# Moving the transposes of an attention pair behind the scores of the next pair in a fused attention and MLP kernel

## The chip, the cores and the metric

The kernel runs on one core of a Trainium2 chip. Its metric is the device time of one execution in microseconds (us), and a kernel's time is the median of several executions. Here the three of the kernel before are 601.35, 600.53 and 597.79 us, so the median is 600.53 us.

## The reference, cut to what matters

Three layers follow each other. The change touches the first alone.

```python
# attention: q, k, v are (2, 8, 768, 64); n_sink 4, window 128
scores = scale * q @ k.T
scores = where(is_sink | in_window, scores, -1e9)
a = exp(scores - max); a = a / (sum(a) + 1e-9)
attn = a @ v                      # per batch and head
x = attn -> (2, 768, 512)
# layer 2, with a layer norm ahead
xn = (x - mean) / sqrt(var + 1e-6) * g_ln
x = x + relu(xn @ w_ch1) @ w_ch2  # 512 -> 2048 -> 512
# layer 3: theta = x @ w_theta, cos and sin, two token mixes, w_ch
```

## The kernel before, in words

The 1536 tokens are cut into six pieces of 256 tokens (two tiles of 128). A row of a tile attends to its own tile, to the tile before and to 16 sink columns. Attention runs per piece over four pairs of heads, as a Python generator that the rest of the kernel advances step by step. Its steps are:

- S, the scores (`scores`, L264): per tile one product for each of the two heads, into two PSUM banks.
- the mask with the row's extremum on VectorE (L378), and the exponential with its row sum on ScalarE (L381), into the tile p.
- T, the transposes (`turn_w`, L428), on TensorE: p is turned into the bank wp, and then ScalarE (L431) and VectorE (L432) split it into two fp16 parts wt. For a piece that has sinks, `turn_sinks` turns 16 more columns (L441, L445, L446).
- F, the product with v (`values`, L464), into the bank pv, which VectorE scales into x (L481).

I write S(2,3) for the scores of heads 2 and 3, and T4 or F4 for the transposes and the product of head 4. Only pieces 0 and 1 (below `TURNED`) are turned on TensorE. The later pieces are turned by the DMA queue and the change leaves them alone.

When all heads of piece 0 are done, VectorE forms the layer norm (`norm`: L580, L591, L595, L598), TensorE turns it (`norm_T`, L611), and layer 2 begins. It goes by units: unit u multiplies with the u-th 128 columns of the first weight (`first`, L645) and the u-th rows of the second (`second`, L692). In units 0 to 7 only piece 0 takes part, in plain fp32, and the attention of piece 1 is interleaved with them. From unit 8 piece 1 joins (L666), which needs its own layer norm.

Weights arrive as 64-bit words, 1 MB per unit. `load_w12` loads f0, f1, f2 and so on (L547) into one of two raw buffers. It turns them into fp32 by L551 and L555 on VectorE and L552 and L554 on ScalarE. A buffer is free for the load after next once its L555 is done. f3 therefore waits for f1's L555, and f4 for f2's.

TensorE's order is the order of the Python code (a manual schedule). On VectorE, ScalarE and the DMA-issuing engine SP a scheduler sets the order when the program is built, by its own times. An engine works through its rows in that order. PSUM has few banks for this: in the units two for S, one for wp and one for pv. The tiles p have four buffers and the q and k tiles two.

Of the kernel before, what the change touches and what calls it, by code (L numbers as in the profile page):

```python
# [19 lines left out]
B, H, S, D = 2, 8, 768, 64  # L20
# [26 lines left out]
READY1 = 5.5  # L47
READY2 = 13.0
RATE = 7.0
PRE = [12, 17, 21]  # L50
AHEAD = (4, 4)
START = 2
EARLY = 38.0
# [14 lines left out]
class Net:  # L68
# [197 lines left out]
    def attn_fast(self, eng):  # L266

        steps = [(piece, h) for piece in range(NP) for h in range(H)]
        nc, p, qk, scored, turned, sent, late = self.nc, self.att, {}, [], [], [], []

        def load(j, eng=eng):
            if j < len(steps):
                piece, h = steps[j]
                if h % 2 == 0:
                    qk[piece, h] = qk[piece, h + 1] = self.split_qk(piece, h // 2, eng)

        def load_v(piece):
            if piece < NP:
                b, tiles = self.tiles(piece)
                for t in ([tiles[0] - 1] if tiles[0] else []) + tiles + ([NT] if tiles[-1] >= 2 else []):  # L280
                    self.split_v(b, t)

        def ahead(piece):
            return self.tc.high_priority() if piece < TURNED else ExitStack()

        def turn():

            piece, h, pt, st = scored.pop(0)
            b, tiles = self.tiles(piece)
            with ahead(piece):  # L290
                blocks = self.turn_w(pt, tiles)
            sinks = None
            if tiles[0]:
                sinks = []
                if not turned:

                    pool, tag = self.vbanks[self.vturn % len(self.vbanks)]
                    self.vturn += 1
                    with ahead(piece):
                        self.turn_sinks(pool.tile([128, 512], F32, tag=tag, name="pv"), pt, sinks)  # L300
            turned.append((piece, h, blocks, sinks, st, pt))

        def finish(head):

            piece, h, blocks, sinks, st = head[:5]
            b, tiles = self.tiles(piece)
            with ahead(piece):
                self.values(b, h, tiles, piece, blocks, sinks, st, turned[0] if turned and turned[0][3] is not None else None)
                if h % (H // 2) == H // 2 - 1:
                    self.stats(piece, h // (H // 2))  # L310
            if h == V_RANGE:
                while late:
                    q, ts = self.tiles(late.pop())
                    for t in ts:
                        with self.behind():
                            self.range_v(q, t)
            if h == H - 1:
                with ahead(piece):
                    self.norm(piece)
                late.append(piece)  # L320

        load(0, self.nc.vector)
        load_v(0)
        for j, (piece, h) in enumerate(steps):
            if h % 2:
                continue
            b, tiles = self.tiles(piece)
            if h == 0:
                self.x[piece] = self.new_x(piece)
            load(j + 2)  # L330
            if h == 2:
                load_v(piece + 1)
            pair = yield from self.softmax(b, (h, h + 1), tiles, qk[piece, h])
            if piece >= TURNED:
                if len(sent) >= LAG:
                    for _ in range(2):
                        finish(sent.pop(0))
                for h, pt, st in pair:
                    sent.append((piece, h) + self.send_w(pt, tiles) + (st,))
                yield  # L340
                continue
            for h, pt, st in pair:
                scored.append((piece, h, pt, st))
                turn()
                yield
                if len(turned) > 2:
                    finish(turned.pop(0))
                    yield
            if h == H - 1:

                while turned:
                    finish(turned.pop(0))
                    yield
        while sent:
            yield
            finish(sent.pop(0))
        for t in tiles:
            self.range_v(b, t)
# [457 lines left out]
    def run(self, general):  # L816
# [47 lines left out]
        while 0 not in self.xnorm:  # L864
            next(side)
            n += 1
            if n == 1:
                self.late()
            if n in PRE and not general:
                with self.behind():  # L870
                    self.load_w12(PRE.index(n))
        if general:
            for f in range(len(PRE)):
                self.load_w12(f)
# [220 lines left out]
```

## Time and profile before

| what | us |
|---|---|
| median of three executions | 600.53 |
| the profiled execution's own time | 601.21 |
| its span, first to last instruction | 599.4 |
| until layer 2 begins (L645 of unit 0) | 48.60 |
| until piece 1 joins (first L666) | 123.65 |

The profiled execution lies 0.7 us above the median, inside the spread of the three. A row of the timeline gives start, duration, engine, line, operation, output and inputs, shapes and count. In brackets stands the time that the engine was idle before it, and who ended that. A row of the waits gives the sum, the number and the longest. A row of grouped instructions gives busy time and the mean of one in ns, then the idle time before them by releaser.

### The profile page before, as it was taken

Reading aid. Unit: us, or ns where it says so; the run is one execution under the profiler, and the core shown is the slowest. Engines: PE = TensorE matmul, PEld = TensorE weight load, DVE = VectorE, ACT = ScalarE, POOL = GpSimd, SP = SyncE. Lnnn points to the kernel's source line nnn. Section 1 sums busy time; section 2 is a strip of 40 time slices with the busy share of each in tenths; the row PEclk is TensorE's granted clock in tenths of the full one; section 3 lists DMA queues with packets and bytes.
Section 4 is the critical chain, followed back from the end, with each engine's and each line's share of the span. In section 5 each row is a group of like instructions: output and inputs, shape, how many; then the busy total and the mean of one; then the engine's idle time right before and its main releaser. Section 6 shows DMA issues by size and latency. Waiting matters only on the chain.

```text
span 599.4 us, 9411 instructions
## 1 busy us (share of the span) xinstructions
PE 545.5 (91%) x3545; PEld 449.0 (75%) x3545; DVE 407.5 (68%) x902; ACT 336.2 (56%) x719; POOL 60.9 (10%) x53
## 2 busy tenths in 40 slices
PE   3646887889999999999999899999999899999995
PEld 1424454567777777777888688888999799999995
DVE  5773557789987897787666643557988789754161
ACT  4755666699765775666446533347676566433020
POOL 1000000000000000000022200002333333310000
PEclk9999889999999999999999799999999799999998
DMA  7461545389632456223412210001313311001112
GB/s 251 166 236 56 200 165 188 109 202 220 116 89 50 104 117 102 45 44 46 114 36 100 95 52 1 1 1 54 105 62 119 110 54 64 13 25 35 37 37 76
DMA packets 54536, 55.37 MB, mean 92 GB/s; under 512 B 39760, under 2 KB 42832, under 8 KB 54480
## 3 DMA queue, kind: packets, MB, share of 16 engines
q1 hardware_dynamic: 54480, 54.67, 31.7%
q8 instruction: 30, 0.49, 0.3%
q14 instruction: 26, 0.21, 0.1%
HBM read 42.08 MB, written 3.15 MB: 75 GB/s over the span
## 4 chain that ended last, share of the span: by engine, by line
PE 65%; DVE 13%; DMA 10%; ACT 8%; issue 3%; POOL 1%; SPq 0%; DVEq 0%; ACTq 0%; POOLq 0%
PE acc L692 18%; PE h L666 16%; PE m L777 12%; DMA raw<-w 5%; PE f L808 5%; PE th L736 3%; PE pv L464 3%; PE s L264 3%; ACT raw L552 2%; PE h L645 2%; DMA raw<-wtok 1%; DVE w L555 1%; ACT w L554 1%; DVE st L555 1%; DMA raw<-wth 1%
## 5 line engine op out<-in xcount | busy, mean ns | idle before, releaser
L634 DVE TENSOR_TENSOR wl<-w,wh 128x512 fp32r<-128x512 f32 x96 | 68.9, 721 | 48.8 <-ACT wh L633 25.9
L633 ACT ACTIVATE wh<-w 128x512 fp32r<-128x512 f32 x96 | 59.8, 627 | 72.3 <-PE acc L692 45.6
L666 PE MATMUL h<-xT,wh 128*128 128x512 f32 (+1 forms) x384 | 93.1, 379 | 0.5 <-ACT p L381 0.5
L666 PEld LDWEIGHTS h<-xT,wh 128*128 128x128 f32 x384 | 66.9, 188 | 14.4 <-ACT p L381 0.7
L692 PE MATMUL acc<-wh,hh 128*128 128x512 f32 x176 | 72.9, 414 | 0.0
L692 PE MATMUL acc<-wl,hh 128*128 128x512 f32 x176 | 69.9, 397 | 0.0
L692 PE MATMUL acc<-wh,hl 128*128 128x512 f32 x176 | 69.8, 397 | 0.0
L381 ACT ACTIVATE p<-p,st 128x272 f32<-128x272 f32 (+1 forms) x96 | 47.3, 493 | 21.3 <-DVE st L378 21.3
L666 PE MATMUL h<-xT,wl 128*128 128x512 f32 (+1 forms) x192 | 48.0, 372 | 0.0
L378 DVE CUSTOM_DVE_ANT_0 p<-s,mask 128x272 f32<-128x272 f32 (+1 forms) x96 | 36.9, 407 | 13.1 <-PE s L264 12.7
L692 PEld LDWEIGHTS acc<-wh,hh 128*128 128x128 f32 x176 | 33.8, 192 | 7.7 <-issue 0.2
L692 PEld LDWEIGHTS acc<-wh,hl 128*128 128x128 f32 x176 | 33.6, 191 | 7.7 <-DVE hl L671 0.3
L666 PEld LDWEIGHTS h<-xT,wl 128*128 128x128 f32 x192 | 34.5, 188 | 6.4
L692 PEld LDWEIGHTS acc<-wl,hh 128*128 128x128 f32 x176 | 33.8, 192 | 6.2 <-DVE wl L634 0.4
L552 ACT ACTIVATE raw<-raw 128x1024 f32<-128x1024 f32 (+2 forms) x36 | 34.3, 952 | 6.2 <-DVE st L551 6.0
L464 PEld LDWEIGHTS <-wt 128*128 128x128 f16 x576 | 22.5, 103 | 15.8 <-issue 10.1
L428 PE MATMUL wp<-ident,p 128*128 128x128 f32 x56 | 13.9, 354 | 21.9 <-ACT p L381 16.7
L593 POOL TENSOR_TENSOR rs<-rs,mhalf 128x2 f32<-128x2 f32 x6 | 5.7, 956 | 251.2 <-ACT rs L592 251.2
L464 PE MATMUL pv<-v,wt 128*128 128x64 f16 x528 | 25.9, 201 | 5.6 <-DVE x L481 5.2
L671 DVE SCALAR_TENSOR_TENSOR hl<-h,hh 128x512 fp32r<-128x512 f32 (+1 forms) x48 | 30.6, 637 | 0.2 <-ACT hh L670 0.2
L554 ACT ACTIVATE st<-raw 128x768 uint16<-128x768 uint16 (+1 forms) x20 | 19.4, 969 | 18.1 <-DMA raw<-wtok 5.0
L670 ACT ACTIVATE hh<-h 128x512 fp32r<-128x512 f32 (+1 forms) x48 | 26.5, 551 | 5.1 <-PE h L666 5.1
(300 smaller groups left out, 1395.2 us busy)
## 6 DMA issues: line engine op xcount, KB each, us to landing
raw<-w SPq DMA_DIRECT2D x16, 1024.0 KB, 4.9
raw<-wtok SPq DMA_DIRECT2D x12, 768.0 KB, 4.2
raw<-qk SPq DMA_DIRECT2D x16, 336.0 KB, 3.0
vr<-vt SPq DMA_DIRECT2D x14, 256.0 KB, 2.9
out_dram<-o SPq DMA_DIRECT2D x24, 128.0 KB, 1.7
raw<-qk SPq DMA_DIRECT2D x8, 272.0 KB, 3.3
raw<-wth SPq DMA_DIRECT2D x4, 512.0 KB, 4.0
raw<-wch SPq DMA_DIRECT2D x4, 512.0 KB, 3.3
```

Source lines behind the costliest of these rows:

```text
L378: self.newest = [nc.vector.tensor_tensor_reduce(out=e, in0=ps[h], in1=self.mask[min(t, 2)], scale=-0.125, scalar=3e38, op0=ALU.add, op1=AL ...
L381: nc.scalar.activation(e, e, AF.Exp, bias=st[:, 0, i:i + 1], scale=-1.0, accum_out=st[:, 1, i:i + 1])]
L464: nc.tensor.matmul(pv[:, i * D:(i + 1) * D], a, m, start=j == 0, stop=j == len(prods) - 1)
L552: nc.scalar.activation(hi.bitcast(F32), hi.bitcast(F32), AF.Copy, scale=2.0 ** -112)
L633: nc.scalar.activation(hi, r, AF.Copy)
L634: nc.vector.tensor_tensor(out=lo, in0=r, in1=hi.bitcast(F32), op=ALU.subtract)
L666: nc.tensor.matmul(ps[:, 0:n], a[:, k * 128:(k + 1) * 128], x[:, k, c], start=m == 0, stop=m == 11)
L670: self.relu[u] = nc.scalar.activation(hh, ps[:, 0:n], AF.Relu)
L671: nc.vector.scalar_tensor_tensor(out=hl, in0=ps[:, 0:n], scalar=0.0, in1=hh.bitcast(F32), op0=ALU.max, op1=ALU.subtract)
L692: nc.tensor.matmul(ps, a[:, c], w, start=m == 0 and n == 0, stop=m == NF - 1 and n == len(prods) - 1)
L777: nc.tensor.matmul(ps, z[i][e][:, c * 128:(c + 1) * 128], w[:, t], start=s == 0 and m == 0 and c % 2 == 0, stop=s == NT - 1 and m == 5 and ...
L808: nc.tensor.matmul(ps, self.w_last[k][e][:, c * 128:(c + 1) * 128], u[k][f], start=m == 0, stop=m == 11)
```

## The change

In pieces 0 and 1 a finished pair is put into `scored` and is turned only when the next pair's scores have been issued; the last pair of a piece is turned right away. Up to one head now waits in `turned` where two did: F follows one T later. `PRE` holds the counts of generator steps at which the loads of f0, f1 and f2 are made, and two of them go up by one.

```diff
-PRE = [12, 17, 21]
+PRE = [13, 18, 21]
...
-            for h, pt, st in pair:
-                scored.append((piece, h, pt, st))
+
+            last = h == H - 2
+            scored += [(piece,) + x for x in pair]
+            while len(scored) > (0 if last else 2):
                 turn()
                 yield
-                if len(turned) > 2:
+                if len(turned) > 1:
                     finish(turned.pop(0))
                     yield
-            if h == H - 1:
-
-                while turned:
-                    finish(turned.pop(0))
-                    yield
+
+            while last and turned:
+                finish(turned.pop(0))
+                yield
```

Below the changed lines every line of the changed kernel stands one further down, so that L429 there is L428 here. The names s, p, wp, wt and pv are those of the steps above.

First place: TensorE at the start of the program, before.

```order
L264 MATMUL s<-raw 128x128 x2
L264 MATMUL s<-raw 128x272 x2
L428 MATMUL wp<-ident,p 128x128 x6
L264 MATMUL s<-raw 128x128 x2
L264 MATMUL s<-raw 128x272 x2
L428 MATMUL wp<-ident,p 128x128 x3
L464 LDWEIGHTS wt
```

The same place now:

```order
L264 MATMUL s<-raw 128x128 x2
L264 MATMUL s<-raw 128x272 x2
L264 MATMUL s<-raw 128x128 x2
L264 MATMUL s<-raw 128x272 x2
L429 MATMUL wp<-ident,p 128x128 x6
L465 LDWEIGHTS wt
L465 MATMUL pv<-v,wt 128x64
```

S(2,3) moved ahead of T0 and T1, and F0 ahead of S(4,5).

Second place: TensorE after the first two units of layer 2, in the attention of piece 1, before. w_332 is f0 and w_444 is f2.

```order
L428 MATMUL wp<-ident,p 128x128 x4
L441 MATMUL pv<-ident,p 16x128 x2
L428 MATMUL wp<-ident,p 128x128 x4
L264 MATMUL s<-raw 128x272 x2
L692 MATMUL acc<-w_332,hh 128x512 x2
L264 MATMUL s<-raw 128x272 x2
L428 MATMUL wp<-ident,p 128x128 x4
L645 MATMUL h<-x_522,w_444 128x256 x4
```

The same place now; w_351 is f0.

```order
L264 MATMUL s<-raw 128x272 x4
L429 MATMUL wp<-ident,p 128x128 x4
L442 MATMUL pv<-ident,p 16x128 x2
L693 MATMUL acc<-w_351,hh 128x512 x2
L429 MATMUL wp<-ident,p 128x128 x4
L465 LDWEIGHTS wt
```

Both tiles of S(2,3) now stand side by side ahead of T0, and L692 of unit 0 stands between T0 and T1 instead of between the two tiles of S.

Third place: VectorE in the last heads of piece 0, before. w_444 is f2 and w_537 is f3.

```order
L551 TENSOR_SCALAR w_444<-raw 128x1024
L206 SCALAR_TENSOR_TENSOR v<-vr,v 128x512
L551 TENSOR_SCALAR w_537<-raw 128x1024
L481 TENSOR_TENSOR x_179<-pv,st 128x2x64
L476 RECIPROCAL st<-st 128x2
L555 SCALAR_TENSOR_TENSOR w_444<-raw,w_444 128x1024
L481 TENSOR_TENSOR x_179<-pv,st 128x2x64
```

The same stretch now; w_448 is f2 and w_537 is f3.

```order
L433 SCALAR_TENSOR_TENSOR wt<-wp,wt 128x384
L556 SCALAR_TENSOR_TENSOR w_448<-raw,w_448 128x1024
L482 TENSOR_TENSOR x_179<-pv,st 128x2x64
L206 SCALAR_TENSOR_TENSOR v<-vr,v 128x512
L433 SCALAR_TENSOR_TENSOR wt<-wp,wt 128x384
L552 TENSOR_SCALAR w_537<-raw 128x1024
L482 TENSOR_TENSOR x_179<-pv,st 128x2x64
L581 BN_STATS bn<-x_179 128x6 x2
```

The first operation on f3, which stood ahead of the scaling (L481) of head 4, now stands ahead of that of head 7, the last before the layer norm.

## Rows read from the trace of the kernel before

**Rows 1.** Windows, three stages: stretch, length, busy us (count) by engine, PEclk, DMA share, GB/s.

```profile
0.00:48.60 48.60, 22.95 (x144) 15.14 (x145) 33.71 (x117) 27.90 (x75) 3.45 (x16) 1.00 0.57 201
48.60:123.65 75.05, 58.52 (x344) 35.69 (x345) 45.18 (x109) 47.87 (x102) 1.20 (x1) 0.93 0.44 150
123.65:599.40 475.75, 464.03 (x3057) 398.16 (x3057) 328.58 (x677) 260.39 (x543) 56.21 (x36) 0.98 0.28 72
```

**Rows 2.** Waits of TensorE from 8 to 48 us.

```profile
PE wp L428 <- ACT p L381: 11.8, 8, 3.2
```

**Rows 3.** Timeline, the attention of piece 0: start, us, engine, line.

```profile
3.06 0.43 SPq L231 DMA_DIRECT2D raw<-qk  x1
...
8.75 0.08 DVE L378 DVE_READ_ACCUMULATOR2_ANT st<- 128x1 f32 x1
...
13.47 1.71 PE L264 MATMUL s<-raw 64*128 64x128 f32 x8
...
19.21 1.71 PE L264 MATMUL s<-raw 64*128 64x128 f32 x8
...
27.79 1.71 PE L264 MATMUL s<-raw 64*128 64x128 f32 x8
```

**Rows 4.** DMA issues at 3.06 us: size, us to landing.

```profile
raw<-qk SPq DMA_DIRECT2D x1, 272.0 KB, 5.4
```

**Rows 5.** Grouped instructions by shape, 0 to 124 us.

```profile
L554 ACT ACTIVATE w<-raw 128x1024 uint16<-128x1024 uint16 x12 | 16.2, 1350 | 0.6 <-DMA raw<-w 0.6
L381 ACT ACTIVATE p<-p,st 128x272 f32<-128x272 f32 x30 | 15.4, 513 | 10.7 <-DVE st L378 10.7
L555 DVE SCALAR_TENSOR_TENSOR w<-raw,w 128x1024 int32<-128x1024 int32 x12 | 14.7, 1222 | 14.0 <-ACT w L554 10.8 <-ACT st L475 1.9 <-ACT raw L552 1.2
L552 ACT ACTIVATE raw<-raw 128x1024 f32<-128x1024 f32 x12 | 13.5, 1126 | 0.0
L378 DVE CUSTOM_DVE_ANT_0 p<-s,mask 128x272 f32<-128x272 f32 x30 | 12.1, 430 | 1.6 <-PE s L264 1.6
L551 DVE TENSOR_SCALAR w<-raw 128x1024 uint16<-128x1024 uint16 x13 | 9.8, 752 | 10.3 <-DMA raw<-w 10.2
L206 DVE SCALAR_TENSOR_TENSOR v<-vr,v 128x512 f16<-128x512 f32 x7 | 4.8, 685 | 0.2 <-ACT wt L431 0.2
L381 ACT ACTIVATE p<-p,st 128x128 f32<-128x128 f32 x8 | 3.1, 394 | 2.1 <-DVE st L378 2.0
```

**Rows 6.** Grouped instructions by shape, 0 to 48 us.

```profile
L432 DVE SCALAR_TENSOR_TENSOR wt<-wp,wt 128x384 f16<-128x384 f32 x8 | 4.3, 547 | 0.3 <-ACT wt L431 0.3
L431 ACT ACTIVATE wt<-wp 128x384 f16<-128x384 f32 x8 | 3.7, 478 | 1.1 <-PE wp L428 1.1
L211 DVE TENSOR_REDUCE vmax<-v 128x1 f32<-128x512 f16 x2 | 1.4, 680 | 0.0
```

**Rows 7.** Timeline, the load of f3 and the end of piece 0.

```profile
29.34 0.38 SPq L547 DMA_DIRECT2D raw<-w  x1
...
35.75 0.75 DVE L551 TENSOR_SCALAR w<-raw 128x1024 uint16<-128x1024 uint16 x1 [2.36 <-DMA raw<-w]
...
40.26 0.29 DVE L481 TENSOR_TENSOR x<-pv,st 128x128 f32<-128x128 f32 x1 [0.73 <-PE pv L464]
...
48.60 5.98 PE L645 MATMUL h<-x,w 128*128 128x256 f32 x16 [0.88 <-DVE x L617]
```

**Rows 8.** Line L547, 0 to 130 us, all 14 loads of weights.

```profile
DMA to landing us min/median/max: 4.6/4.8/7.6
```

**Rows 9.** Waits of TensorE from 48 to 124 us.

```profile
PE wp L428 <- DVE wt L432: 5.2, 2, 4.0
PE wp L428 <- ACT p L381: 5.0, 3, 2.2
PE s L264 <- DVE st L378: 3.1, 2, 1.7
PE pv L464 <- DVE x L481: 2.4, 2, 1.2
```

## The prediction

> **What bounds the kernel now.** I read the windows first. TensorE is busy for 464.0 of the 475.8 us after piece 1 joins, so that stage has at most 11.8 us of idle time. Before it, TensorE is busy for 22.9 of 48.6 us and then for 58.5 of 75.1 us [rows 1]. The two early stages hold 42 us of idle time, and all that the change moves lies in them. From unit 8 on the order of TensorE's rows is the same. So what the early stages gain should reach the end nearly whole: a full TensorE only starts its long stretch sooner.
>
> Next come TensorE's waits. In piece 0 the transposes waited for the exponentials eight times, 11.8 us in all [rows 2]. In the units four waits matter: the transposes for the bank wp, which the split (L432) has to empty, 5.2 us; the transposes for the exponentials, 5.0; the scores for the masks, 3.1; F for the scaling L481, 2.4 [rows 9].
>
> Then the timeline. S(2,3), S(4,5) and S(6,7) start at 13.47, 19.21 and 27.79 [rows 3], each behind transposes that waited. Last the weights: VectorE waited 10.2 us in L551 for weights to land, in a queue where attention work stands behind [rows 5].
>
> **The change, piece 0.** The number of instructions is the same; only places change.
>
> S(2,3) now needs its inputs, which land at 3.06 + 5.4 = 8.5 [rows 3, 4], and two banks, which the masks of the first tile leave at 8.8 [rows 3]. So its first tile starts at 8.9 instead of 13.47. The second tile needs the banks of the first pair's second tile. That is two masks of 0.43 and two splits of v of 0.69 after 8.75 [rows 3, 5]: 11.0. The two maxima of v (0.68 each [rows 6]) that stood between them are placed later now.
>
> That lead isn't kept whole, since the first split (L431) now stands behind four exponentials of the next pair. These take 2 x 0.39 + 2 x 0.51 = 1.8 us on ScalarE [rows 5] and I let them end at 13.6, because their masks follow each other from 11.0 on. Then L431 0.48, L432 0.55 [rows 6] and F0 (0.7, an estimate from VectorE's wait of 0.73 for one F [rows 7]) give 15.4 for S(4,5) instead of 19.21. The same walk through the next pair, with F1 and F2 ahead of S(6,7), gives about 21 instead of 27.79. So far the change is worth 6.8 us.
>
> The price stands behind it. S(6,7) ends at 22.7, but VectorE has L555 of f0 (1.22), two splits of v (0.69 each), L432 (0.55) and the four masks to do [rows 5, 6], some 4.7 us, and the last exponential of the pair ends near 27.2. ScalarE's new order puts the conversion of f1 behind it: L554 1.35, L552 1.13, with a short one between, to 29.7; L555 1.22 [rows 5] to 30.9. Before, f1's buffer was free at 29.34, when f3 was issued [rows 7]. So f3's load goes out 1.6 us later than before, though everything else is early. Before, it took 6.4 us (29.34 to 35.75). So f3 lands at 37.3, L551 takes 0.75, and L481 of head 7, which stands behind it on VectorE (third place), starts at 38.0 instead of 40.26 [rows 7]: 2.3 us sooner. Behind L481 one split of v (0.69 [rows 5]) is gone from the way to the layer norm. **Piece 0 gains 2.3 + 0.7 = 3.0 us.** With the shortest landing, 4.6 [rows 8], it would be 1.8 more: 4.8. At the other end, if ScalarE gets to f1 three us later than reckoned, it is 0.
>
> At 35.75 the row shows VectorE idle for 2.36 us in a load's first operation, with L481 next in the queue [rows 7]. [...]
>
> **The change, units 0 to 7.** What goes: the transposes find their exponentials done, since a pair of scores and a unit's product lie between: 5.0. T1 finds wp empty, because L692 of unit 0 stands between T0 and T1 (second place) and covers L432; likewise later pairs: 5.2. F6 and F7 no longer follow each other directly: 2.4. Together 12.6 [rows 9]. The 3.1 for scores lies in piece 2, and stays.
>
> What comes: no product stands between the two tiles of S any longer, while the units have two banks for scores. The second tile waits for two masks, 0.86 us [rows 5], and for whatever VectorE has ahead of them. Three pairs, each between 0.9 and the longest such wait of 1.7 [rows 9]: 2.7 to 5.1. I take 4.4, since L551 and L555 stand near these masks. And wp is still one bank: where two T have only F between them, ScalarE's conversion of a weight (1.35 + 1.13 [rows 5]) stands ahead of L431. I count two such waits of 1.5 us, between nothing and the 4.0 of the longest [rows 9]: 3.0. **The units gain 12.6 - 4.4 - 3.0 = 5.2 us.** The bounds are 0, if each wait comes back in another place, and 12.6 - 2.7 = 9.9.
>
> Edits that I cost at nothing: `PRE` (f0, f1 and f2 keep their rank among the loads of SP, which waits for buffers there and not for the step), and the maxima of v, 1.4 us of VectorE moved into the units, where it is busy for 45.2 of 75.1 us [rows 1]. If that cover fails they cost 1.4.
>
> **The sum.** 601.2 (the profiled execution's own time) - 3.0 - 5.2 = 593.0. The median of the runs shown lies 0.7 below that execution, so I forecast 592.5 us. Its own range, from the bounds with about half of each, is 589 to 597. About 1%, or 6 us, is what a measurement of this kernel can tell from no change.
>
> **The rivals.**
>
> *The units give nothing back* (0.20). Each wait of TensorE only changes its name: p for the masks, wt for wp. For it: VectorE waited 10.8 us for ScalarE in L555 [rows 5], a bound that the order of TensorE doesn't touch. Against it: TensorE's idle time was at T and F, which now have cover. Only piece 0's 3.0 is left: 598.2, or 597.5 as a median.
>
> *Nothing is gained at all* (0.10). f3's load takes as long as the longest, 7.6 [rows 8], and its buffer is free a little later than I reckon; units as above. 600.5.
>
> *VectorE's queue is held by loads, and the kernel is slower* (0.07). The place is L551: the one of f3 ahead of the last scaling of piece 0, and those of the next six weights among the masks and splits of piece 1. The waits were 10.2 us in six cases, 1.7 each [rows 5]. TensorE's work is early now but the loads aren't, so each of six could wait 1.7 longer, 10.2 in all. If nothing but piece 0's 3.0 stands against that, it comes to 601.2 + 10.2 - 3.0 = 608.4, or 607.5. It begins to decide when f3 lands after 40.26 - 0.75 = 39.5 [rows 7], 2.2 us later than I say: then the layer norm of piece 0 is later than before.
>
> *The clock stays up, and it is faster still* (0.13). In the units the granted clock is 0.93 on average [rows 1]. [...]
>
> [...] I keep it at 0.13, since my walk leaves TensorE more than 8 us of waits.
>
> **How the numbers follow.** The forecast has 0.50, the rivals 0.20, 0.10, 0.07 and 0.13. Faster by over 1% means below 594.5: most of the forecast's own spread (0.42 of 0.50) and the clock rival, 0.55. Within 1%: the rest of the forecast, 0.08, and the two cases without much gain, 0.30, so 0.38. Slower by over 1%: 0.07. The range for 8 in 10 reaches from the clock rival to the case in which only piece 0 gains, 587 to 599; it leaves out the slower case and parts of the ends.
>
> **What would show it.** Right: in the changed trace S(2,3) starts near 9, S(4,5) near 15.5, S(6,7) near 21; VectorE waits in the L551 of f3 right before the last L481 of piece 0; L645 of unit 0 starts near 45.6 (48.60 before [rows 7]); the waits of T for exponentials are nearly gone in the units, and new ones of 1 to 2 us stand at the second tiles of S; the first L666 comes near 115.5 instead of 123.65. Wrong: L645 of unit 0 starts at 48 or later, or the stage from there to the first L666 still takes 75 us, or the time after the first L666 isn't 476 us as before.

## The result, and the profile after

The changed kernel takes 591.58 us (median of four executions, 589.16 to 593.17), the kernel before 599.68 in the same comparison (four, 597.79 to 601.35). The ratio is 0.9864 with a 95% interval of 0.9833 to 0.9894, so it is faster by 1.1 to 1.7%. The forecast was 592.5 us. A second comparison of the same two kernels (e9 below) gave 0.9886 [0.9852, 0.992].

The profiled execution took 593.17 us, with a span of 591.3. Lines stand one further down than before. The windows by stage answer to [rows 1], with the same columns:

```profile
0.00:44.93 44.93, 24.25 (x144) 16.08 (x145) 32.00 (x114) 26.89 (x74) 3.67 (x16) 1.00 0.60 212
44.93:116.29 71.36, 60.71 (x344) 39.53 (x345) 46.29 (x110) 48.12 (x101) 1.31 (x1) 0.90 0.47 158
116.29:591.30 475.01, 462.17 (x3059) 396.02 (x3057) 329.77 (x679) 261.05 (x546) 56.28 (x36) 0.99 0.28 73
```

Layer 2 begins 3.7 us sooner (44.93 for 48.60), the units take 3.7 us less (71.36 for 75.05), and the rest is 475.0 us for 475.8. In the units TensorE's idle time fell from 16.5 to 10.7 us, by 5.9. But its busy time rose from 58.5 to 60.7 us, though it runs as many products. The granted clock reads 0.90 on average and not 0.93, and the slow rows below show where the time went.

TensorE's waits from 8 to 48 us, to be read against [rows 2]:

```profile
PE pv L465 <- DVE x L482: 3.7, 3, 1.7
PE tp L612 <- DVE xn L599: 3.5, 1, 3.5
PE pv L465 <- ACT wt L432: 3.0, 3, 2.0
...
```

The 11.8 us in which the transposes waited for exponentials are gone from this list; what is left are F's waits for the scaling (3.7) and for ScalarE's half of wt (3.0), and the one for the layer norm (3.5). TensorE's timeline of piece 0, against [rows 3]:

```profile
8.68 1.08 PE L264 MATMUL s<-raw 64*128 64x128 f32 x4 [0.54 <-DVE st L379]
9.94 2.23 PE L264 MATMUL s<-raw 64*128 64x272 f32 x4 [0.17 <-DVE st L379]
...
15.11 1.71 PE L264 MATMUL s<-raw 64*128 64x128 f32 x8
...
21.93 1.71 PE L264 MATMUL s<-raw 64*128 64x128 f32 x8
...
36.41 2.19 PE L264 MATMUL s<-raw 64*128 64x272 f32 x8
42.09 1.97 PE L612 MATMUL tp<-ident,xn 128*128 128x128 f32 x8 [3.49 <-DVE xn L599]
```

S(6,7) leads its old place by 5.9 us (21.93 for 27.79), but layer 2 by 3.7 only. It would have led by more, had a load of v landed sooner. ScalarE waited 1.10 us for that load in L204, with a split of wt behind it, and F2, which stands ahead of S(6,7), waited for the split:

```profile
19.29 0.63 ACT L204 ACTIVATE v<-vr 128x512 f16<-128x512 f32 x1 [1.10 <-DMA vr<-vt]
20.85 0.29 PE L465 MATMUL pv<-v,wt 128*128 128x64 f16 x2 [2.02 <-ACT wt L432]
```

Where the lead was lost is seen on VectorE, against [rows 7]:

```profile
30.68 1.23 DVE L556 SCALAR_TENSOR_TENSOR w<-raw,w 128x1024 int32<-128x1024 int32 x1 [0.22 <-ACT raw L553]
...
36.77 0.75 DVE L552 TENSOR_SCALAR w<-raw 128x1024 uint16<-128x1024 uint16 x1 [0.90 <-DMA raw<-w]
37.41 0.28 DVE L482 TENSOR_TENSOR x<-pv,st 128x128 f32<-128x128 f32 x1
```

The first row is f1's last conversion, which frees the buffer at 31.9. SP's row shows that f3's load goes out right then:

```profile
31.94 3.07 SPq L548 DMA_DIRECT2D raw<-w  x2
```

It lands 4.8 us later, VectorE sits idle for 0.90 us in L552 until then, and the last scaling of piece 0 follows behind it in the queue. Ahead of that, VectorE had hardly a gap, as the window from 28 to 36 us shows (its 7.00 us busy are the third of the engines' times):

```profile
28.00:36.00 8.00, 4.03 (x37) 2.83 (x37) 7.00 (x15) 6.23 (x11) 0.00 (x0) 1.00 0.62 227
```

In the units, [rows 9] become:

```profile
PE s L264 <- DVE st L379: 8.2, 6, 2.1
PE wp L429 <- DVE wt L433: 2.4, 2, 1.3
```

The sum of the four waits is 10.6 us where it was 15.7. Two are gone, and the one of the scores grew from 3.1 to 8.2. The timeline shows where:

```profile
53.03 1.08 PE L264 MATMUL s<-raw 64*128 64x272 f32 x4 [0.97 <-DVE st L379]
...
62.58 1.08 PE L264 MATMUL s<-raw 64*128 64x272 f32 x4 [1.97 <-DVE st L379]
63.60 3.21 PE L693 MATMUL acc<-w,hh 128*128 128x512 f32 x4
...
76.07 0.72 PE L264 MATMUL s<-raw 64*128 64x272 f32 x2 [1.52 <-DVE st L379]
77.20 0.72 PE L264 MATMUL s<-raw 64*128 64x272 f32 x2 [0.41 <-DVE st L379]
77.86 3.67 PE L646 MATMUL h<-x,w 128*128 128x256 f32 x8
...
87.88 3.40 PE L646 MATMUL h<-x,w 128*128 128x256 f32 x8
...
106.34 3.09 PE L646 MATMUL h<-x,w 128*128 128x256 f32 x8
```

The second tile of each pair of S waits until the masks have emptied its two banks: 0.97 + 1.97 + 1.52 + 0.41 = 4.87 us. Four rows of products are slow: L693 takes 3.21 us at 63.60, and L646 takes 3.67, 3.40 and 3.09, where such rows take 1.88 and 1.89 us elsewhere in the stage. Before, there were three:

```profile
60.79 3.30 PE L692 MATMUL acc<-w,hh 128*128 128x512 f32 x4
...
80.52 3.58 PE L692 MATMUL acc<-w,hh 128*128 128x512 f32 x4
...
103.99 3.17 PE L645 MATMUL h<-x,w 128*128 128x256 f32 x8
```

Above 1.9 us each, the slow rows come to 5.8 us now and 4.4 before. The first 16 products of the stage took 6.47 us at 44.93 where they took 5.98 [rows 7]. Together that is 1.9 of the 2.2 us by which the busy time rose. What the one more slow row comes from, these rows don't show.

### The profile page after: what moved, and what is told of

It is laid out like the page before. It is cut to its first block, busy times and chain, and to the rows that moved or that the text cites. A ratio compares the mean times of both kernels' runs of the same rounds, so it can differ in the third digit from the quotient of the medians.

```text
span 591.3 us, 9409 instructions
## 1 busy us (share of the span) xinstructions
PE 547.1 (93%) x3545; PEld 451.6 (76%) x3545; DVE 408.1 (69%) x902; ACT 336.1 (57%) x719; POOL 61.3 (10%) x53
## 4 chain that ended last, share of the span: by engine, by line
PE 56%; DVE 17%; ACT 13%; DMA 8%; issue 3%; POOL 1%; SPq 0%; DVEq 0%; ACTq 0%; POOLq 0%
PE acc L693 18%; PE h L667 17%; PE m L778 6%; PE f L809 5%; PE s L264 3%; ACT raw L553 3%; PE h L646 3%; DMA raw<-w 2%; PE pv L465 2%; DVE st L556 2%; ACT w L555 2%; PE th L737 2%; DMA raw<-wtok 1%; DVE w L556 1%; ACT p L382 1%
## 5 line engine op out<-in xcount | busy, mean ns | idle before, releaser
L667 PE MATMUL h<-xT,wh 128*128 128x512 f32 (+1 forms) x384 | 93.3, 379 | 0.0
L667 PEld LDWEIGHTS h<-xT,wh 128*128 128x128 f32 x384 | 66.8, 188 | 14.1 <-issue 0.8
L693 PE MATMUL acc<-wh,hh 128*128 128x512 f32 x176 | 72.4, 411 | 0.0
L693 PE MATMUL acc<-wl,hh 128*128 128x512 f32 x176 | 69.3, 394 | 0.0
L693 PE MATMUL acc<-wh,hl 128*128 128x512 f32 x176 | 69.0, 392 | 0.0
L667 PE MATMUL h<-xT,wl 128*128 128x512 f32 (+1 forms) x192 | 48.0, 372 | 0.0
L667 PEld LDWEIGHTS h<-xT,wl 128*128 128x128 f32 x192 | 34.4, 188 | 6.4
L693 PEld LDWEIGHTS acc<-wh,hh 128*128 128x128 f32 x176 | 33.4, 190 | 7.5 <-issue 0.2
L693 PEld LDWEIGHTS acc<-wh,hl 128*128 128x128 f32 x176 | 33.3, 189 | 7.6 <-DVE hl L672 0.2
L693 PEld LDWEIGHTS acc<-wl,hh 128*128 128x128 f32 x176 | 33.4, 190 | 6.1 <-DVE wl L635 0.4
L556 DVE SCALAR_TENSOR_TENSOR w<-raw,w 128x1024 int32<-128x1024 int32 x16 | 19.6, 1225 | 20.3 <-ACT w L555 16.1
```

Source lines behind the costliest of these rows:

```text
L556: nc.vector.scalar_tensor_tensor(out=dst, in0=hi, scalar=3, in1=dst, op0=ALU.logical_shift_left, op1=ALU.bitwise_or)
L667: nc.tensor.matmul(ps[:, 0:n], a[:, k * 128:(k + 1) * 128], x[:, k, c], start=m == 0, stop=m == 11)
L693: nc.tensor.matmul(ps, a[:, c], w, start=m == 0 and n == 0, stop=m == NF - 1 and n == len(prods) - 1)
```

## The experiments

Each is compared with the kernel before, run on the same chip in the same comparison (medians of before: 598.47 us for e1 to e4, 599.97 for e5 to e8, 598.66 for e9 to e11).

**The change in piece 0 alone, and in piece 1 alone.** e1 is the changed kernel with the old order in piece 1, e2 the one with the old order, and the old `PRE`, in piece 0. The cut shows e1; e2 has `if piece == 1` there.

```diff
+            if piece == 0:
+                last = h == H - 2
+                scored += [(piece,) + x for x in pair]
...
+            else:
+                for h, pt, st in pair:
+                    scored.append((piece, h, pt, st))
+                    turn()
...
```

> The new order in piece 0 alone; piece 1 has the order of before. My theory (the two gains are separate and add up): L645 of unit 0 starts near 44.9 us as in the changed kernel, the stage from there to the first L666 takes 75 us as before, and the time is 3.7 us below before, ratio near 0.994. Rival (the weights pace the units, so that a lead of piece 0 is lost while units wait for weights): the first L666 still comes near 123.6 and the ratio is within 0.002 of 1.

> The new order in piece 1 alone; piece 0 has the order of before. My theory: L645 of unit 0 starts near 48.6 us as before, the stage to the first L666 takes 71.4 us instead of 75.0, the transposes no longer wait for exponentials there, three waits of 1 to 2 us stand at the second tiles of the scores, and the ratio is near 0.994. Rival (the stage got shorter only because its weights were there when it began earlier): the stage takes 75 us and the ratio is within 0.002 of 1.

Measured: e1 596.23 us, ratio 0.9938 [0.9911, 0.9964]; e2 589.01 us, 0.9833 [0.9797, 0.987]. The windows of e1, then of e2:

```profile
0.00:44.87 44.87, 24.51 (x144) 16.11 (x145) 33.55 (x117) 27.27 (x75) 3.67 (x16) 1.00 0.60 213
44.87:123.11 78.24, 63.24 (x345) 39.50 (x345) 45.44 (x109) 47.79 (x102) 1.04 (x1) 0.87 0.44 146
```

```profile
0.00:47.13 47.13, 22.93 (x144) 15.18 (x145) 32.51 (x114) 27.17 (x74) 3.84 (x16) 1.00 0.59 202
47.13:117.78 70.65, 59.48 (x345) 38.12 (x345) 45.29 (x106) 46.99 (x97) 1.14 (x1) 0.90 0.46 156
```

Both parts gain alone. e1 begins layer 2 3.7 us sooner, as the whole change does, but its units take 3.2 us more than before, where I had expected no change: 1.5 us less idle time and 4.7 more busy time, at a granted clock of 0.87. So by the time piece 1 joins (123.11), only 0.5 us of the lead is left in this profile. The rival had that place right, but not its reason, since the idle time fell. The ratio came as I had it. e2 shortens the units by 4.4 us. Its ratio is far below the 0.994 that I expected. It also begins layer 2 1.5 us sooner, which I hadn't expected either: as in the whole change, the scheduler now puts the two maxima of v (L211) and a split of v behind the start of layer 2 (114 operations of VectorE in the first stage, not 117 as in e1 and before). The gains don't add: by the medians 2.2 us for e1 and 9.5 for e2 against 8.1 for the whole, by the ratios 3.7, 10.0 and 8.2. The stage behind the first L666, which the edits leave alone, takes 472 to 476 us in the profiles of this document, and e2's has 473.0, so some of its gain in the profile (590.8 for 599.4) lies there and not in the units.

**e3: F one later, and nothing else** (the kernel before).

```diff
-                if len(turned) > 2:
+                if len(turned) > 1:
```

> The kernel before with the second part of the change alone: F stands one transpose behind its own, not two; scores and transposes keep their order. My theory (the gain is in the transposes, which wait for exponentials, not in F): piece 0 is within 1 us of before, since S(2,3) still stands behind T0 and T1; the waits of transposes for exponentials in piece 0 stay near 11.8 us; ratio 0.997 to 1.003. Rival (F placed earlier is what frees the bank pv and the layer norm): L645 of unit 0 starts 2 us or more earlier, ratio below 0.996.

Measured: 596.88 us, 0.9966 [0.9943, 0.9989]. Its waits of TensorE in the units:

```profile
PE s L264 <- DVE st L378: 5.8, 6, 2.1
PE wp L428 <- DVE wt L432: 5.5, 3, 3.4
```

My theory had the place of layer 2 right (48.48, as before), but not the waits: in piece 0 the transposes still waited for exponentials, but for 7.3 us where it was 11.8. The ratio lies just below my range. In the units this edit too puts the two tiles of S side by side, so their wait grows, while the one for wp stays. The greater part of the gain needs the transposes behind the next scores, for this edit alone is worth 0.3% and the whole 1.4%.

**e4: f3's conversion behind piece 0's layer norm** (the changed kernel; `normed` is the last L599).

```diff
-                self.newest = [self.relu[u]]
+                self.newest = [self.relu[u]] + ([self.normed] if u == 0 else [])
```

> The changed kernel with the conversions of f3 and f4 on VectorE held until the layer norm of piece 0 is done, so that no load stands ahead of the last scaling. My theory (the lead of S(6,7) is lost at the load of f3): the wait of 0.9 us and the two operations of 0.75 us leave the way to the layer norm, L645 of unit 0 starts 1.5 to 2.4 us earlier, near 43; the time gains what the units don't lose again by the later conversions, ratio to before 0.981 to 0.986. Rival (VectorE is full there anyway, or F7 sets the end): L645 starts within 0.5 us of 44.9.

Measured: 589.09 us, 0.9834 [0.9793, 0.9874]. On its VectorE the last scaling of piece 0, with no load ahead of it (f3's first operation comes at 40.24):

```profile
35.65 0.29 DVE L482 TENSOR_TENSOR x<-pv,st 128x128 f32<-128x128 f32 x1 [0.65 <-PE pv L465]
```

Without f3 in its way L482 comes 1.8 us sooner (35.65 for 37.41) and waits for F alone; layer 2 begins at 43.68, 1.25 us sooner. S(6,7), which f3 doesn't touch, was 0.86 us earlier already in this execution (21.07 for 21.93), as L204 waited 0.3 us for the load of v where it was 1.10, and F2 waited 1.22 us for the split where it was 2.02. So f3 accounts for 0.9 us at L482, the length of VectorE's wait. At layer 2 it is less: from S(6,7) to the first L646 it takes 22.61 us here and 23.00 in the changed kernel, so f3 was worth 0.4 us there, and not the 1.5 to 2.4 that I expected. So its load did stand on the way to the layer norm, but it took only 0.9 of the 3.0 us that were lost between S(6,7) (ahead by 5.86 us) and L482 (by 2.85). The other 2 us lie in the stretch in which VectorE is busy 7.0 of 8 us with the conversions of f1 and f2 among the last heads; that these are the reason is argued and no run takes them out. Against the changed kernel's 0.9864 the time itself can't be told apart.

**e5: the maxima of v behind piece 0's layer norm** (the kernel before).

```diff
-                        with self.behind():
+                        with self.tc.issue_after(self.normed.ins if hasattr(self.normed, 'ins') else self.normed):
```

> The kernel before with nothing but the two maxima of v (L211) held behind the layer norm of piece 0. In the second experiment they stood later too, by a side effect, and L645 of unit 0 started 1.5 us earlier at an unchanged order of TensorE. Theory now: these 1.4 us of VectorE are on the way to the layer norm; L645 starts between 46.8 and 47.6 us, ratio 0.996 to 0.999. Rival (VectorE has room there, as the prediction had it; the 1.5 us came from another shift of the scheduler): L645 within 0.4 us of 48.6.

Measured: 599.17 us, 0.9997 [0.9974, 1.002]; layer 2 begins at 46.91, 1.7 us sooner, as I had it, but the time is that of before, and the ratio lies above my range. So the move of the maxima alone is worth nothing that can be measured here (the interval leaves room for 1.6 us), and the profile's early lead of 1.7 us isn't seen in the median. In the new order of piece 0 the move isn't needed for an early layer 2: in e1 the maxima stand where they stood before, and layer 2 begins at 44.87.

**e6: a transpose between the two tiles of S** (the changed kernel, piece 1 only; `mid` is `turn`). **e7** is e6 and e4 together. **e8** is the changed kernel with `START = 3` for 2: one more step of piece 1's attention is taken ahead of layer 2, so that a product of a unit comes between the two tiles of the later pairs.

```diff
+            if piece == 1 and len(turned) > 1:
+                finish(turned.pop(0))
+                yield
...
+            if mid and i == 0:
+                mid()
+                yield
         for h, pt, st in pair:
```

So an F, too, moves up to right behind the scores of the pair.

> The changed kernel with one transpose of the pair before put between the two tiles of scores in piece 1. My theory (the second tile waits for two masks because nothing stands between): the three waits in the units, 0.97, 1.97 and 1.93 us, each fall by about 0.6, the length of a transpose, or go; the stage from L645 of unit 0 to the first L666 has some 2 us less idle time than the 10.7 of the changed kernel; ratio to before 0.981 to 0.987. Rival (the wait is for VectorE's queue and only moves to the next transpose, whose bank is emptied later): idle time in the stage within 0.7 us of 10.7, the waits of transposes for L432 grow by as much.

> The sixth and the fourth edit together. If the two gains are separate: L645 of unit 0 near 43.7 us, the stage near 66 us, ratio to before 0.976 to 0.982, and better than either alone. If the transposes between the scores give nothing: the ratio of the fourth experiment, 0.983.

> The changed kernel with one more step of attention ahead of layer 2 (START 3 instead of 2), so that a unit's product (1.9 us) stands between the two tiles of scores, as in the kernel before. My theory: the three waits of 1 to 2 us at the second tiles go below 0.5 us each, idle time in the stage falls by 3 us or more; L645 of unit 0 starts up to 1 us later, since four more products and masks stand ahead of the layer norm; ratio to before 0.979 to 0.988. Rival (as above, VectorE's queue sets the pace): the idle time stays within 1 us of 10.7 and stands at the transposes instead.

Measured: e6 583.76 us, 0.9711 [0.9688, 0.9735]; e7 582.77 us, 0.9708 [0.9683, 0.9733]; e8 593.51 us, 0.9886 [0.9863, 0.9909]. The window of the units in e6:

```profile
44.59:109.10 64.51, 58.18 (x345) 37.49 (x345) 46.05 (x108) 46.83 (x100) 1.15 (x1) 0.88 0.53 175
```

Its timeline of TensorE at the first two pairs of the units, where L435 are the transposes and L699 is the second product:

```profile
50.74 0.73 PE L264 MATMUL s<-raw 64*128 64x272 f32 x4
51.40 0.66 PE L435 MATMUL wp<-ident,p 128*128 128x128 f32 x4
...
52.69 1.08 PE L264 MATMUL s<-raw 64*128 64x272 f32 x4 [0.41 <-DVE st L382]
...
59.43 0.73 PE L264 MATMUL s<-raw 64*128 64x272 f32 x4
60.09 0.66 PE L435 MATMUL wp<-ident,p 128*128 128x128 f32 x4
60.58 1.88 PE L699 MATMUL acc<-w,hh 128*128 128x512 f32 x4
62.40 0.73 PE L264 MATMUL s<-raw 64*128 64x272 f32 x4
```

With one transpose (and in the second and third pair a product of the unit as well) between the tiles, their wait falls from 4.87 to 0.41 us, and the units from 71.36 to 64.51: 4.3 us less idle time and 2.5 less busy time. That is twice the idle time that I had expected, and the ratio lies below my range. In e7 layer 2 begins at 45.13 and not near 43.7, since F2 waited 2.74 us for the split of ScalarE and S(6,7) came at 22.53; the 22.60 us from S(6,7) on are those of e4. In e8 the second tiles no longer wait in the units, as I had it, but its idle time there is 10.0 us, as the rival had it. The waits only moved, as its list for the units shows:

```profile
PE pv L465 <- ACT wh L634: 3.3, 2, 2.2
PE wp L429 <- DVE wt L433: 3.2, 2, 2.8
PE s L264 <- DVE st L379: 2.2, 1, 2.2
```

(The 2.2 us there lie in piece 2.) So a product between the tiles isn't enough by itself; which of the differences between e6 and e8 decides wasn't tried. e6 and e7 beat both kernels; between the two nothing can be told.

**e9 to e11: the sizes again.** e9 is the changed kernel unaltered, e10 is e2 unaltered, e11 is e6 with piece 0 in its old order.

> The changed kernel itself once more, beside the next two on the same chip, since the second experiment (piece 1 alone) was no slower than the whole change. Both theories: ratio near 0.986, as before.

> The second experiment once more. Theory now: piece 0's part of the change moves L645 of unit 0 by 2.2 us (44.9 against 47.1 us), and piece 1's part with the later maxima gives the rest; so this kernel is 1 to 3 us slower than the changed one, ratio 0.987 to 0.992. Rival (piece 0's part is worth nothing on top of the rest, because a denser start of the units costs clock): equal to the changed kernel within 1 us, ratio near 0.985 or below.

> The sixth experiment's order in piece 1 (a transpose between the two tiles of scores), with piece 0 in the order of before. Theory: L645 of unit 0 starts 2 to 3 us later than in the sixth experiment (44.6 us), the stage behind it is as short (64 to 66 us), and the ratio is 0.974 to 0.977 against 0.971 there. Rival (piece 0's part is worth nothing on top): ratio 0.971 as there.

Measured: e9 591.93 us, 0.9886 [0.9852, 0.992]; e10 588.45 us, 0.9834 [0.9787, 0.9881]; e11 584.26 us, 0.9763 [0.9731, 0.9794]. The window of the units in e9:

```profile
45.66:114.67 69.01, 59.23 (x345) 38.32 (x345) 46.28 (x110) 48.20 (x101) 1.33 (x1) 0.93 0.48 163
```

Piece 0's part on top of piece 1's brings nothing that these runs show (e9 against e10), as the rival for e10 had it. In the profiles layer 2 begins at 45.66 and 46.06, so here piece 0's part moved it by 0.4 us, and not by the 2.2 of the changed kernel against e2. e11 came as the theory for it had it: a ratio within its range, and layer 2 at 47.10, 2.5 us later than in e6; only its units, 61.7 us, are shorter than the 64 to 66 that I expected. By the ratios e6 gains some 3 us over e11, by the medians 0.5, on different chips; their intervals just overlap. So whether piece 0's part is worth anything on top stays open. The same kernel's units took 71.36 us at 0.90 in one profile and 69.01 at 0.93 in another, so differences of 2 us in that stage are within what two executions differ by.

## Why the prediction was right

**Piece 0, forecast 3.0 us, measured 3.7 and 2.9.** The walk held. S(2,3) was to start at 8.9 and 11.0 and started at 8.68 and 9.94 (the second tile starts behind the first of its two masks, and one of the two splits of v stands behind that mask); S(4,5) was to start at 15.4 and did at 15.11; S(6,7) at 21 and did at 21.93. For the last the walk left out the load of v, for which L204 waited 1.10 us, with the split behind it that F2 needs. In the changed kernel, e4, e6, e7 and e9 F2 waited 2.02, 1.22, 1.41, 2.74 and 2.85 us for that split, and S(6,7) came at 21.93, 21.07, 21.41, 22.53 and 22.61, each time 0.9 to 1.1 us behind F2's start. The rest of the lead was lost on VectorE, as the text has it: ahead of the last scaling, in a stretch that the conversions fill, and then in L551 of f3. Two sizes were off and nearly cancel, which is luck: f1's conversion ended at 31.9 and not 30.9, and f3 took 4.8 us to land, near the shortest, where I took the 6.4 of the one before. L481 of head 7 came at 37.41 for 38.0, and L645 of unit 0 at 44.93 for 45.6, in e9 at 45.66. From there to layer 2 it was 7.5 us instead of 8.3, so the split of v that is gone was worth 0.8 for 0.7.

The lead of S(6,7) didn't reach the layer norm whole: 5.9 us became 2.9 at L482. In the changed kernel the last product of F7 ends at 36.49 and L482 starts at 37.41, behind L552 of f3; in e4, with f3 out of that queue, the product ends at 35.61 and L482 starts at 35.65, and 0.9 us of the lead came back. But the prediction made too much of this one load: its walk had a gain of 6.8 us up to S(6,7) and let it end at the load of f3; without f3 in the way e4 shows layer 2 4.9 us sooner than before, e7 3.5.

**The units, forecast 5.2 us, measured 3.7 and 6.0.** The waits went as written. Of the 12.6 us that were to go, the ones for exponentials (5.0) and for the scaling (2.4) went whole; the one for wp was to leave 3.0 and left 2.4. The second tiles of S were to cost 4.4 and cost 4.87. The four rows of waits fell by 15.7 - 10.6 = 5.1 us, and all idle time by 5.9. So what missed in this profile is that these pass into the stage unchanged: the term left out TensorE's own pace. In windows of 1 us the clock of the units reads 1.00 but for stretches of 3.4 us at 0.50. There are three of them before (from 60.1, 80.6 and 104.4 us), 10.2 us in all, and four in the changed kernel (from 64.2, 77.9, 88.1 and 105.2), 13.6. Each of the slow rows falls on one of them: L646 takes 3.67 us at 77.86 for 1.89 elsewhere. So I estimate that half of the time at 0.50 is lost, of the 3.4 us more 1.7, and with the 0.5 of the slower first products that is the 2.2 us by which the busy time rose. In e9, at 0.93, the busy time rose by 0.7 and the stage fell by 6.0. So the forecast of 5.2 lies between two profiles of one kernel, and what is left of the miss is no larger than their difference.

**The sum.** 601.2 - 3.0 - 5.2 = 593.0 was forecast for the profiled execution, which took 593.17; the first L667 came at 116.29 (115.5 forecast; 114.67 in e9), and the stage behind it took 475.0 us (476). That the sum fits to 0.2 us is in part luck: piece 0 gave 0.7 more than forecast, the units 1.5 less and the rest 0.7 more. The shape of the sum holds without it, since the two profiles of the changed kernel end at 8 and 11 us below the one of before. In e5 the moved maxima cost nothing either, and with the old `PRE` in the changed kernel the instructions stand in the same order on every engine, so that edit moves nothing.

**The rivals.** That the units give nothing back fell with the 5.1 us of waits. That nothing is gained needed f3's landing to take 7.6 us; it took 4.8. That loads hold VectorE needed waits in L551 longer by 10.2; over the first 130 us they are now shorter, 5.5 us in eight cases where there were 11.4 in seven:

```profile
  DVE w L552: 5.5, 8
```

That the clock stays up in the units is not what happened: it reads 0.90 and 0.93, with a third or more of the idle time gone, and read 0.93 before [rows 1]. The lower end of the range, 587, takes 5.3 us off the forecast, as a loss to the clock in the units that was to go. No run shows this term; what the traces show is 10.2 us at 0.50 in the units before, of which 5.1 are lost by the estimate above, and 13.6 in the changed kernel, so that the loss grew and didn't go. In the windows of the units 16.5 us of idle time went with 0.93 before, 10.7 with 0.90 in the changed kernel and 9.8 with 0.93 in e9. The three runs with the least idle time, 6.3 in e6, 7.2 in e7 and 6.8 in e11, read 0.88, 0.95 and 0.93, and e6's counts a start at 0.53, as shown at the end. So from the kernel before to the changed one less idle time went with no higher clock. Over all the runs a link between the two is neither shown nor excluded.

**What stays open.** The parts don't add: piece 1's alone gains as much as both. e1 and e2 show each gain alone and e9 and e10 show that the two together bring no more than e2's, but the loss isn't traced to a wait: the profiles of e9 and e10 (spans of 588.5 and 590.1 us) stand the other way round than their medians. Why the units' products run slower in one execution than in another is open as well. A third raw buffer, which would let f3 go out early, wasn't tried.

## What to carry to other kernels

A lead on one engine can be lost in another engine's queue: here 5.9 us on TensorE were 2.9 behind the last scaling on VectorE and 3.7 at layer 2. So look for the loads that stand in that queue (here f3 on VectorE, which waited 0.90 us for it, and v on ScalarE, 1.10) and ask when each goes out and lands. When a consumer is moved behind the next producer, two producers may come to stand side by side on the same banks, as the tiles of S do here, where the second ones waited 4.87 us; put the moved work between them, as e6 does (0.41 us), and not behind both. Judge a stage by idle and busy time apart, since two profiles of one kernel differ here by 2.4 us in the units, of which 1.5 are busy time.

## What the runs showed of the hardware

The granted clock of the first stage reads 1.00 in most of these profiles, but products of one shape differ there in their durations. The changed kernel's S(4,5) and S(6,7) take 1.71 us each, for eight products of one shape. In e6 S(4,5) takes 1.71 and S(6,7) 0.95:

```profile
15.39 1.71 PE L264 MATMUL s<-raw 64*128 64x128 f32 x8
21.41 0.95 PE L264 MATMUL s<-raw 64*128 64x128 f32 x8
36.05 2.19 PE L264 MATMUL s<-raw 64*128 64x272 f32 x8
```

e6's windows of the same time and of the start of its units (columns as in [rows 1]):

```profile
10.00:20.00 10.00, 8.23 (x43) 5.20 (x42) 7.23 (x33) 7.63 (x30) 0.00 (x0) 1.00 0.87 295
20.00:30.00 10.00, 5.33 (x44) 3.56 (x45) 8.68 (x25) 8.44 (x20) 0.00 (x0) 0.62 0.58 194
30.00:40.00 10.00, 5.11 (x38) 3.25 (x37) 8.19 (x22) 5.08 (x12) 0.70 (x1) 0.50 0.72 245
45.00:50.00 5.00, 5.00 (x14) 3.96 (x14) 0.00 (x0) 1.62 (x3) 0.00 (x0) 0.53 0.00 0
```

At 36.05 the recorded clock is 0.50, and S of piece 1 takes 2.19 us. It takes the same 2.19 in the changed kernel at 36.41, where the column reads 1.00. So these products were as slow there as at a recorded 0.50, and in these two profiles a 1.00 ahead of the first other reading doesn't show how fast they ran. It bears on the units. In the changed kernel the same 5 us read 1.00:

```profile
45.00:50.00 5.00, 5.00 (x12) 4.01 (x13) 0.00 (x0) 1.28 (x2) 0.00 (x0) 1.00 0.00 0
```

Yet the first 16 products took 6.47 us there and 6.21 in e6. So e6's 0.88 for its units counts a slow start that the changed kernel's 0.90 and the 0.93 of before leave out; without those 5 us at 0.53 e6's 0.88 would be 0.91, by my estimate, and the changed kernel reads 0.89 from 52 us on.
